# Two matmul bursts of a scan made one: the B^T x products of a Mamba-2 chunk scan written beside its C.B products

## The chip, the cores and the metric

The kernel runs on one core of a Trainium2 chip. A core has a matrix engine (TensorE, PE in the profile; its weight loads are PEld), a vector engine (DVE), a scalar engine (ACT), GpSimd (POOL) and a sync engine (SP) that issues DMAs. Each engine takes its own instructions in the order in which they were written. Matmul results land in PSUM, which has eight banks of 2 KB in each of 128 partitions; everything else lies in SBUF. The metric is the device time of one execution in microseconds (us).

## The reference

A chunked state-space scan feeds a feed-forward layer. All is float32, four sequences of 768 steps, 8 heads, head size 32, state size 16. The recurrence is linear, so the chunk length is a choice of the kernel.

```python
for c in range(nc):                                  # per chunk, every batch b and head h
    cum = np.cumsum(log_a[chunk]); L = exp(cum_i - cum_j) * causal
    CB = einsum('bhin,bhjn->bhij', Cc, Bc)
    y_intra = einsum('bhij,bhjd->bhid', CB * L, xc)
    y_inter = einsum('bhin,bhnd->bhid', Cc, state) * exp(cum)
    y[chunk] = y_intra + y_inter
    Bx = Bc (outer) xc * exp(cum_last - cum)
    state = exp(sum(la)) * state + sum_j(Bx)
x = y as (3072, 256)
h = x @ w_in                                         # 256 -> 2048
out = (h * sigmoid(h)) @ w_out                       # 2048 -> 256
```

## The kernel before, in words

The 3072 rows are cut into 12 units of 256 steps, three to a sequence; a unit holds four chunks of 64 steps. The kernel works on three units at a time: in round g it runs the first layer of unit g (`f_s1`), the scan of unit g+1, and the second layer of unit g-2 (`f_s2`). A round has eight slots j, and in each slot the code writes down, in this order, an eighth of `f_s1`, a piece of the scan, in the first two rounds a piece of the weights (`next_w`), and from round 2 on an eighth of `f_s2`. No scheduler reorders it. So the order in the code is the order in every engine's queue, and semaphores hold an instruction until its inputs are there and its buffer is free.

The scan of a unit has five pieces. `f_P` and `f_E` (slot 0) make the decays on DVE with some small POOL steps; `f_T` and `f_B` (slot 1) transpose B and C on PE and scale B by the decays on POOL (the tile BT); `f_G` (slot 2) forms the C.B products, 16 matmuls into the four PSUM banks of the tile gy, and DVE multiplies them by the decays (the tile M); `f_D` (slot 4) forms the B^T x products, 16 matmuls (12 in the last unit of a sequence), and DVE runs the state recurrence over them (the tiles st, then sp); `f_Y` (slot 6) forms the scan's output, 16 (or 12) matmuls from sp and 32 from M, and ACT copies it to SBUF as XM, the input of `f_s1` one round later.

PSUM is full: the pool `ps_s` has one buffer of four banks (gy, shared in turn by the C.B products and the scan's output), `ps_h` has two buffers of one bank (hp), and `ps_o` two for the second layer. hp serves the first layer's results, the transposes and the B^T x products in turn. `f_D` takes both hp buffers at once, one for each half c of the 128 partitions of x (L278 writes `dp[c]`).

The weights are not used as they arrive. Each of 16 pieces (8 of w_in, 8 of w_out) passes ACT (L136, L138), POOL (L141), DVE (L146), POOL (L147) and DVE (L152) in the first two rounds, one piece per slot and step.

A float32 matmul shows up as two records in the trace, so 16 matmuls are 32 records, and an eighth of a layer (four matmuls of 256 columns) is 8 records.

Of the kernel before, what the change touches and what calls it, by code (L numbers as in the profile page):

```python
# [7 lines left out]
FP32 = mybir.dt.float32  # L8
# [11 lines left out]
def kernel(  # L20
# [20 lines left out]
    nc = tc.nc  # L41
# [5 lines left out]
    UPB = S // UT  # L47
# [15 lines left out]
    ps_h = ctx.enter_context(tc.tile_pool(name="ps_h", bufs=2, space=bass.MemoryType.PSUM))  # L63
# [5 lines left out]
    pa, ab, bct, xt = {}, {}, {}, {}  # L69
# [130 lines left out]
    for i in range(2):  # L200
        t = const.tile([128, UT], FP32, name=f"pb{i}")
# [3 lines left out]
    E, M, BT, BH, CE, CW, PFX, ST, DP, XM, GTS, OPS = ({} for _ in range(12))  # L205


    def f_P(u):

        t, s = pa.pop(u), pb[u % 2]  # L210
        nc.vector.tensor_scalar(out=t, in0=t, scalar1=1.0, scalar2=1e-6, op0=ALU.min, op1=ALU.max)  # L211
        starts = t.rearrange("p (c t) -> p c t", t=Q)[:, :, 0:1]
        nc.gpsimd.tensor_copy(out=s.rearrange("p (c t) -> p c t", t=Q)[:, :, 0:1], in_=starts)  # L213
        nc.gpsimd.memset(starts, 0.0)
        PFX[u] = sc.tile([128, UT], FP32, name="pfx")
        nc.vector.tensor_tensor_scan(out=PFX[u], data0=t, data1=s, initial=0.0, op0=ALU.mult, op1=ALU.add)

    def f_E(u):
        t = ab.pop(u)
        nc.vector.tensor_scalar(out=t, in0=t, scalar1=1.0, scalar2=1e-6, op0=ALU.min, op1=ALU.max)  # L220
        nc.gpsimd.memset(t[:, :, :, 0:1], 0.0)  # L221
        E[u] = sc.tile([128, 2, H, Q], FP32, name="E")
        nc.vector.tensor_tensor_scan(out=E[u].rearrange("p k h t -> p (k h t)"),  # L223
                                     data0=t.rearrange("p k h t -> p (k h t)"),
                                     data1=diag.rearrange("p g t -> p (g t)"),
                                     initial=0.0, op0=ALU.mult, op1=ALU.add)

    def f_B(u):

        BT[u] = sc.tile([128, 2, H, N], FP32, name="BT")  # L230
        nc.gpsimd.tensor_tensor(out=BT[u], in0=bct[u][:, 0], in1=E[u][:, :, :, Q - 1:Q].to_broadcast([128, 2, H, N]),
                                op=ALU.mult)

    def f_T(u):

        tp = ps_h.tile([128, 4, 128], FP32, name="hp")
        for i in range(2):
            for k in range(2):
                nc.tensor.transpose(out=tp[:, 2 * i + k], in_=bct[u][:, i, k].rearrange("p h n -> p (h n)"),  # L239
                                    identity=ident)  # L240
        BH[u] = sc.tile([128, UT], FP32, name="bh")
        CE[u] = sc.tile([128, 2, UT], FP32, name="ce")
        CW[u] = sc.tile([128, UT], FP32, name="cw")
        tb = tp[:, 0:2].rearrange("p k t -> p (k t)")
        tcc = tp[:, 2:4].rearrange("p k t -> p (k t)")
        nc.scalar.activation(BH[u], tb, AF.Copy)
        for e in range(2):
            nc.scalar.activation(CE[u][:, e], tcc, AF.Copy, scale=par[:, e:e + 1])  # L248
        nc.vector.tensor_tensor(out=CW[u], in0=tcc, in1=PFX[u], op=ALU.mult)  # L249

    def f_G(u):
        bh, ce = BH.pop(u), CE.pop(u)
        gram = ps_s.tile([128, 4, 512], FP32, name="gy")
        for k in range(2):
            for c in range(2):
                ts = slice(128 * k + 64 * c, 128 * k + 64 * c + 64)
                for g in range(4):
                    nc.tensor.matmul(out=gram[64 * c:64 * c + 64, g, 128 * k:128 * k + 128],  # L258
                                     lhsT=bh[32 * g:32 * g + 32, ts], rhs=ce[32 * g:32 * g + 32, :, ts],
                                     start=True, stop=True, tile_position=(32 * g, 64 * c), skip_group_check=True)  # L260
        M[u] = sc.tile([128, 2, 4, 2 * Q], FP32, name="M")
        nc.vector.tensor_tensor(out=M[u].rearrange("p k g x -> p g k x"),  # L262
                                in0=gram[:, :, 0:256].rearrange("p g (k x) -> p g k x", k=2),
                                in1=E[u].rearrange("p k (g e) t -> p g k (e t)", e=2), op=ALU.mult)

    def f_D(u):

        first, last = u % UPB == 0, u % UPB == UPB - 1
        bt = BT.pop(u).rearrange("p k h n -> p k (h n)")
        xc = xt[u].rearrange("p k h d -> p k (h d)")  # L270
        E.pop(u)
        bct.pop(u)
        dp = [ps_h.tile([128, 512], FP32, name="hp") for c in range(2)]
        n = 3 if last else 4
        for t in range(n):
            k, c = divmod(t, 2)
            for g in range(4):
                nc.tensor.matmul(out=dp[c][32 * g:32 * g + 32, 64 * k:64 * k + 64],  # L278
                                 lhsT=bt[64 * c:64 * c + 64, k, 32 * g:32 * g + 32],
                                 rhs=xc[64 * c:64 * c + 64, k, 64 * g:64 * g + 64], start=True, stop=True,  # L280
                                 tile_position=(64 * c, 32 * g), skip_group_check=True)
        if first:
            ST[u] = sc.tile([128, 4, 64], FP32, name="st")
        if not last:
            ST[u + 1] = sc.tile([128, 4, 64], FP32, name="st")
        for t in range(n):
            k, c = divmod(t, 2)
            o = ST[u][:, t + 1] if t < 3 else ST[u + 1][:, 0]
            d = dp[c][:, 64 * k:64 * k + 64]
            if first and t == 0:  # L290
                nc.vector.tensor_copy(out=o, in_=d)
            else:
                nc.vector.scalar_tensor_tensor(out=o, in0=ST[u][:, t], scalar=PFX[u][:, Q * t + Q - 1:Q * t + Q],  # L293
                                               in1=d, op0=ALU.mult, op1=ALU.add)

        s0 = 1 if first else 0
        sp = DP[u] = sc.tile([128, 4, 64], FP32, name="sp")
        nc.vector.tensor_tensor(out=sp[:, s0:], in0=ST.pop(u)[:, s0:],  # L298
                                in1=hmask.rearrange("p e d -> p (e d)").rearrange("p (o x) -> p o x", o=1)
                                .to_broadcast([128, 4 - s0, 64]), op=ALU.mult)  # L300
        PFX.pop(u)

    def f_Y(u):
        first = u % UPB == 0
        sp, cw, m, xc = DP.pop(u), CW.pop(u), M.pop(u), xt.pop(u)
        m = m.rearrange("p k g (e t) -> p k (g e) t", e=2)

        y = ps_s.tile([128, 4, 512], FP32, name="gy")
        for t in range(1 if first else 0, 4):
            k, c = divmod(t, 2)  # L310
            for g in range(4):
                w, q = divmod(g, 2)
                nc.tensor.matmul(out=y[64 * q:64 * q + 64, 2 * w + c, 64 * k:64 * k + 64],  # L313
                                 lhsT=sp[32 * g:32 * g + 32, t], rhs=cw[32 * g:32 * g + 32, Q * t:Q * t + Q],
                                 start=(k == 0 or (first and t == 2)), stop=False,
                                 tile_position=(32 * g, 64 * q), skip_group_check=True)
        for k in range(2):
            for w in range(2):
                for c in range(2):
                    for q in range(4):  # L320
                        h = 4 * w + q
                        nc.tensor.matmul(out=y[32 * q:32 * q + 32, 2 * w + c, 64 * k:64 * k + 64],  # L322
                                         lhsT=xc[64 * c:64 * c + 64, k, h], rhs=m[64 * c:64 * c + 64, k, h],
                                         start=False, stop=True, tile_position=(64 * c, 32 * q),
                                         skip_group_check=True)

        XM[u] = sc.tile([128, 4, 128], FP32, name="XM")
        nc.scalar.activation(XM[u], y[:, :, 0:128], AF.Copy)
# [31 lines left out]
    def scan_piece(u, j):  # L360
        if j == 0:
            f_P(u)
            f_E(u)
        elif j == 1:
            f_T(u)
            f_B(u)
        elif j == 2:
            f_G(u)
        elif j == 4:
            f_D(u)  # L370
        elif j == 6:
            f_Y(u)
        elif j == 7 and u + 2 < NU:
            load_unit(u + 2)
# [4 lines left out]
    f_T(0)  # L379
    f_B(0)  # L380
    next_w(0)
    f_G(0)
    next_w(1)
    f_D(0)
    next_w(2)
    f_Y(0)
    next_w(3)
# [42 lines left out]
```

## Time and profile before

| what | value |
|---|---|
| time, median of 3 runs (range) | 435.57 us (435.03 to 436.4) |
| time of the profiled execution | 433.9 us |
| its span, first to last instruction | 432.2 us |
| PE busy | 385.3 us, 89% of the span |
| DVE / ACT / POOL busy | 113.8 / 106.9 / 71.2 us |
| mean granted TensorE clock | 0.988 of 2.4 GHz |
| first layer, PE (L339) | 187.9 us in 768 records |
| second layer, PE (L350) | 181.7 us in 768 records |
| B^T x products, PE (L278) | 8.5 us in 352 records, 9.9 us idle before them |
| POOL, in 40 slices of the span | busy in the first 8, idle after |

"Idle before" is the time in which the engine stood still just ahead of these instructions. The profile has two stages: a ramp of some 89 us in which the weights are prepared, and a stage of some 310 us in which each round repeats.

### The profile page before, as it was taken

How to read it: one execution, taken by the hardware profiler on the slowest of the kernel's cores; microseconds unless marked ns; L12 is line 12 of the kernel's file. 1: busy time of each engine (PE TensorE's matmuls, PEld its weight loads, DVE VectorE, ACT ScalarE, POOL GpSimd, SP SyncE). 2: the span in 40 equal slices, each digit the busy share in tenths (PEclk: the TensorE clock that was granted, in tenths of full speed). 3: DMA queues.
4: the chain of work that ended last, by engine and by line, in shares of the span. 5: the costliest groups of instructions: out<-in, count | busy, mean ns of one | idle time of the engine just before them, and what ended most of it. 6: DMA issues, size and time to landing. Idle time of an engine off the chain costs nothing.

```text
span 432.2 us, 7900 instructions
## 1 busy us (share of the span) xinstructions
PE 385.3 (89%) x3440; PEld 323.9 (75%) x3440; DVE 113.8 (26%) x162; ACT 106.9 (25%) x202; POOL 71.2 (16%) x95
## 2 busy tenths in 40 slices
PE   2255785799999999999999999999999999999996
PEld 1144563688888888888888888887887887888885
DVE  1728868813212213113014014014014011000000
ACT  2254564131221222222222221221222221221000
POOL 4567988500000000000000000000000000000000
PEclk9998998899999999999999999999999999999999
DMA  9969469402502403303304305205200000000101
GB/s 160 170 222 198 164 170 198 52 0 51 73 14 66 57 14 75 48 14 79 51 6 89 47 3 94 42 2 93 44 0 14 14 2 12 14 9 4 24 14 24
DMA packets 110082, 26.20 MB, mean 61 GB/s; under 512 B 101344, under 2 KB 105952, under 8 KB 110048
## 3 DMA queue, kind: packets, MB, share of 16 engines
q1 hardware_dynamic: 103808, 25.18, 29.0%
q10 hardware_dynamic: 6240, 0.52, 1.2%
q8 instruction: 27, 0.44, 0.4%
q14 instruction: 7, 0.06, 0.1%
HBM read 22.54 MB, written 3.15 MB: 59 GB/s over the span
## 4 chain that ended last, share of the span: by engine, by line
PE 79%; POOL 9%; DMA 4%; SPq 2%; issue 2%; ACT 2%; ACTq 1%; DVE 1%; POOLq 0%; DVEq 0%
PE o_ps L350 40%; PE hp L339 34%; POOL wu L141 6%; POOL wv L147 3%; PE gy L322 2%; DMA xt<-in_x_dram 2%; PE gy L313 1%; PE gy L258 1%; ACT gT L341 1%; DMA raw<-in_moe_w_in_dram 1%; SPq L93 1%; PE hp L239 1%; PE hp L278 1%; DMA ab<-in_a_dram 1%; ACTq L93 1%
## 5 line engine op out<-in xcount | busy, mean ns | idle before, releaser
L339 PE MATMUL hp<-XM,w_in_sb 128*128 128x256 f32 x768 | 187.9, 390 | 20.2 <-DVE w_in_sb L152 6.2
L339 PEld LDWEIGHTS hp<-XM,w_in_sb 128*128 128x128 f32 x768 | 149.4, 196 | 43.7 <-issue 9.5
L350 PE MATMUL o_ps<-w_out_sb,gT 128*128 128x256 f32 x768 | 181.7, 383 | 0.0
L350 PEld LDWEIGHTS o_ps<-w_out_sb,gT 128*128 128x128 f32 x768 | 143.0, 190 | 21.2 <-issue 1.5
L341 ACT ACTIVATE gT<-hp 128x512 f32<-128x512 f32 x96 | 57.2, 596 | 231.0 <-PE hp L339 231.0
L249 DVE TENSOR_TENSOR cw<-hp,pfx 128x256 f32<-128x256 f32 x12 | 5.0, 421 | 124.0 <-ACT ce L248 124.0
L213 POOL COPY pb<-pa 128x4 f32<-128x4 f32 x12 | 2.3, 191 | 207.2 <-DVE pa L211 207.2
L141 POOL TENSOR_SCALAR wu<-wu 128x512 f32<-128x512 f32 x16 | 32.8, 2054 | 6.4 <-ACT wu L136 6.4
L223 DVE TENSOR_TENSOR_SCAN E<-ab,diag 128x1024 f32<-128x1024 f32 x12 | 28.3, 2355 | 2.6 <-POOL ab L221 2.6
L293 DVE SCALAR_TENSOR_TENSOR st<-st,pfx,hp 128x64 f32<-128x64 f32 x40 | 11.2, 281 | 43.5 <-PE hp L278 41.8
L147 POOL TENSOR_TENSOR wv<-wu,wv 128x512 uint32<-128x512 uint32 x16 | 21.3, 1333 | 3.2 <-DVE wu L146 3.2
L355 ACT ACTIVATE o_sb<-o_ps 128x256 f32<-128x256 f32 x24 | 9.2, 383 | 49.8 <-PE o_ps L350 49.8
L262 DVE TENSOR_TENSOR M<-gy,E 128x1024 f32<-128x1024 f32 x12 | 14.7, 1223 | 24.6 <-PE gy L258 24.6
L146 DVE TENSOR_SCALAR wu<-wu 128x512 uint32<-128x512 uint32 x16 | 16.8, 1053 | 12.4 <-POOL wu L141 12.4
L278 PE MATMUL hp<-xt,BT 64*32 64x64 f32 x352 | 8.5, 234 | 9.9 <-ACT gT L341 6.5
L278 PEld LDWEIGHTS hp<-xt,BT 64*32 64x32 f32 x352 | 4.7, 109 | 15.7 <-ACT gT L341 8.3
L136 ACT ACTIVATE wu<-raw 128x512 f32<-128x512 f32 x16 | 10.7, 669 | 16.1 <-DMA raw<-in_moe_w_in_dram 12.7
L239 PE MATMUL hp<-ident,bct 128*128 128x128 f32 x48 | 8.2, 288 | 6.9 <-DMA bct<-in_B_dram 4.0
L313 PEld LDWEIGHTS gy<-cw,sp 32*64 32x64 f32 x352 | 6.5, 138 | 8.5 <-issue 8.5
L138 ACT ACTIVATE wv<-raw 128x512 f32<-128x512 uint32 x16 | 10.6, 666 | 8.7 <-DVE w_out_sb L152 5.6
L239 PEld LDWEIGHTS hp<-ident,bct 128*128 128x128 f32 x48 | 6.2, 145 | 8.7 <-DMA bct<-in_C_dram 3.2
L313 PE MATMUL gy<-cw,sp 32*64 32x64 f32 x352 | 8.2, 230 | 4.6 <-DVE sp L298 4.6
(33 smaller groups left out, 116.9 us busy)
## 6 DMA issues: line engine op xcount, KB each, us to landing
ab<-in_a_dram SPq DMA_DIRECT2D x48, 128.0 KB, 4.0
raw<-in_moe_w_in_dram SPq DMA_DIRECT2D x8, 512.0 KB, 6.8
raw<-in_moe_w_out_dram SPq DMA_DIRECT2D x8, 512.0 KB, 4.4
out_dram<-o_sb SPq DMA_DIRECT2D x48, 64.0 KB, 1.9
xt<-in_x_dram SPq DMA_DIRECT2D x22, 128.0 KB, 3.0
pa<-in_a_dram SPq DMA_DIRECT2D x12, 128.0 KB
bct<-in_B_dram SPq DMA_DIRECT2D x22, 64.0 KB, 3.6
bct<-in_C_dram SPq DMA_DIRECT2D x22, 64.0 KB, 3.5
```

Of the source, the lines that this page charges most:

```text
L141: nc.gpsimd.tensor_scalar(out=u, in0=u, scalar1=LEAST, scalar2=MOST, op0=ALU.max, op1=ALU.min)
L146: nc.vector.tensor_scalar(out=u, in0=u, scalar1=3, scalar2=None, op0=ALU.logical_shift_left)
L147: nc.gpsimd.tensor_tensor(out=v, in0=u, in1=v, op=ALU.add)
L223: nc.vector.tensor_tensor_scan(out=E[u].rearrange("p k h t -> p (k h t)"), data0=t.rearrange("p k h t -> p (k h t)"), data1=diag.rearrange ...
L239: nc.tensor.transpose(out=tp[:, 2 * i + k], in_=bct[u][:, i, k].rearrange("p h n -> p (h n)"), identity=ident)
L262: nc.vector.tensor_tensor(out=M[u].rearrange("p k g x -> p g k x"), in0=gram[:, :, 0:256].rearrange("p g (k x) -> p g k x", k=2), in1=E[u] ...
L278: nc.tensor.matmul(out=dp[c][32 * g:32 * g + 32, 64 * k:64 * k + 64], lhsT=bt[64 * c:64 * c + 64, k, 32 * g:32 * g + 32], rhs=xc[64 * c:64 ...
L293: nc.vector.scalar_tensor_tensor(out=o, in0=ST[u][:, t], scalar=PFX[u][:, Q * t + Q - 1:Q * t + Q], in1=d, op0=ALU.mult, op1=ALU.add)
L313: nc.tensor.matmul(out=y[64 * q:64 * q + 64, 2 * w + c, 64 * k:64 * k + 64], lhsT=sp[32 * g:32 * g + 32, t], rhs=cw[32 * g:32 * g + 32, Q ...
L339: nc.tensor.matmul(out=hp[:, i], lhsT=w_in_sb[:, kc, f * 128:(f + 1) * 128], rhs=xm[:, kc], start=(kc == 0), stop=(kc == KC - 1))
L341: nc.scalar.activation(GTS[g][:, 2 * j:2 * j + 2], hp, AF.Silu)
L350: nc.tensor.matmul(out=OPS[g], lhsT=GTS[g][:, f, 128 * c:128 * c + 128], rhs=w_out_sb[:, f, :], start=(f == 0), stop=(f == NF - 1))
```

## The change

The B^T x matmuls no longer get buffers of their own. The C.B products fill columns 0 to 255 of each 512-column bank of the tile gy; the B^T x products of half c now go into columns 256 to 383 of bank c of the same tile. Both sets of matmuls are issued as one burst in slot 2 (`f_GD`), and DVE then does M, st and sp one behind the other. The scan's output burst (`f_Y`) moves from slot 6 to slot 5. Ahead of the rounds, for unit 0, the one burst stands where `f_D` stood.

```diff
-    def f_G(u):
+    def f_GD(u):
...
         gram = ps_s.tile([128, 4, 512], FP32, name="gy")
...
+        for t in range(n):
+            k, c = divmod(t, 2)
+            for g in range(4):
+                nc.tensor.matmul(out=gram[32 * g:32 * g + 32, c, 256 + 64 * k:320 + 64 * k],
+                                 lhsT=bt[64 * c:64 * c + 64, k, 32 * g:32 * g + 32],
+                                 rhs=xc[64 * c:64 * c + 64, k, 64 * g:64 * g + 64], start=True, stop=True,
+                                 tile_position=(64 * c, 32 * g), skip_group_check=True)
         M[u] = sc.tile([128, 2, 4, 2 * Q], FP32, name="M")
...
-    def f_D(u):
...
-        dp = [ps_h.tile([128, 512], FP32, name="hp") for c in range(2)]
...
-                nc.tensor.matmul(out=dp[c][32 * g:32 * g + 32, 64 * k:64 * k + 64],
...
-            d = dp[c][:, 64 * k:64 * k + 64]
+            d = gram[:, c, 256 + 64 * k:320 + 64 * k]
...
-            f_G(u)
-        elif j == 4:
-            f_D(u)
-        elif j == 6:
+            f_GD(u)
+        elif j == 5:
             f_Y(u)
...
-    f_G(0)
     next_w(1)
-    f_D(0)
+    f_GD(0)
     next_w(2)
```

On PE, in a round with all three parts (round 2, slot 4 before), the B^T x matmuls L278 stand between the two layers, in two parts with a wait for ACT between them:

```order
L339 MATMUL hp<-XM,w_in_sb 128x256 [waits Activation_49]
L339 MATMUL hp<-XM,w_in_sb 128x256 x3
L278 MATMUL hp<-xt,BT 32x64 [waits DMAHW0_49,Activation_49,Pool_49]
L278 MATMUL hp<-xt,BT 32x64 x3
L278 MATMUL hp<-xt,BT 32x64 [waits Activation_49]
L278 MATMUL hp<-xt,BT 32x64 x3
L278 MATMUL hp<-xt,BT 32x64 [waits DMAHW1_49]
L278 MATMUL hp<-xt,BT 32x64 x7
L350 MATMUL o_ps<-w_out_sb,gT 128x256 x4
L339 MATMUL hp<-XM,w_in_sb 128x256 [waits DVE_49,PE_49]
```

In the changed kernel they stand in slot 2 of the same round, right behind the C.B matmuls (L263, L258 before), and are L269; first and second layer are L337 and L348:

```order
L263 MATMUL gy<-ce,bh 64x128 [waits Activation_49]
L263 MATMUL gy<-ce,bh 64x128 x15
L269 MATMUL gy<-xt,BT 32x64 [waits DMAHW0_49,Pool_49]
L269 MATMUL gy<-xt,BT 32x64 x7
L269 MATMUL gy<-xt,BT 32x64 [waits DMAHW1_49]
L269 MATMUL gy<-xt,BT 32x64 x7
L348 MATMUL o_ps<-w_out_sb,gT 128x256 [waits DVE_49]
L348 MATMUL o_ps<-w_out_sb,gT 128x256
L348 MATMUL o_ps<-w_out_sb,gT 128x256 [waits DVE_49]
```

The B^T x matmuls have lost both waits for ACT and keep those for POOL (BT) and for the load of x.

On DVE, in the ramp (round 0, slots 2 to 4, unit 1), the state recurrence (st, sp) stood behind four steps of the weights, two of L146 and two of L152:

```order
L262 TENSOR_TENSOR M<-gy,E 128x4x2x128 [waits DVE_49,PE_49]
L146 TENSOR_SCALAR wu<-wu 128x512 [waits Pool_49]
L152 SCALAR_TENSOR_TENSOR w_in_sb<-raw,wv 128x2x256 [waits DMAHW2_49,Pool_49]
L146 TENSOR_SCALAR wu<-wu 128x512 [waits DVE_49,Pool_49]
L152 SCALAR_TENSOR_TENSOR w_in_sb<-raw,wv 128x2x256 [waits DMAHW3_49,Pool_49]
L293 SCALAR_TENSOR_TENSOR st<-st,pfx,hp 128x64 [waits PE_49]
L293 SCALAR_TENSOR_TENSOR st<-st,pfx,hp 128x64 [waits DVE_49,PE_49]
L293 SCALAR_TENSOR_TENSOR st<-st,pfx,hp 128x64 [waits DVE_49] x2
L298 TENSOR_TENSOR sp<-st,hmask 128x256
```

Now it stands right behind M, ahead of these steps; the first st has no wait for PE of its own, so the wait of M is for the whole burst:

```order
L274 TENSOR_TENSOR M<-gy,E 128x4x2x128 [waits DVE_49,PE_49]
L291 SCALAR_TENSOR_TENSOR st<-st,pfx,gy 128x64
L291 SCALAR_TENSOR_TENSOR st<-st,pfx,gy 128x64 [waits DVE_49] x3
L296 TENSOR_TENSOR sp<-st,hmask 128x256
L146 TENSOR_SCALAR wu<-wu 128x512 [waits Pool_49]
L152 SCALAR_TENSOR_TENSOR w_in_sb<-raw,wv 128x2x256 [waits DMAHW2_49,Pool_49]
L146 TENSOR_SCALAR wu<-wu 128x512 [waits Pool_49]
L152 SCALAR_TENSOR_TENSOR w_in_sb<-raw,wv 128x2x256 [waits DMAHW3_49,Pool_49]
```

Of a unit's DVE steps in the ramp, st and sp moved up past four steps of the weights.

## Rows read from the trace of the kernel before

**Rows 1.** Windows: us, PE, PEld, DVE, ACT, POOL busy (instructions), granted clock, DMA, GB/s

```profile
88.71:399.00 310.29, 306.33 (x2696) 260.37 (x2695) 57.21 (x92) 69.13 (x135) 8.48 (x32) 1.00 0.20 36
68.30:73.50 5.20, 5.17 (x20) 4.07 (x20) 4.53 (x4) 2.56 (x5) 5.20 (x5) 0.70 0.85 245
```

**Rows 2.** Waits of PE from 92 to 400 us: total, times, longest

```profile
PE hp L278 <- ACT gT L341: 4.0, 9, 0.4
```

**Rows 3.** Timeline of PE, round 2, and its end: start, us, records, [idle before <- releaser]

```profile
96.15 0.69 PE L258 MATMUL gy<-ce,bh 32*64 32x128 f32 x32
96.77 1.99 PE L350 MATMUL o_ps<-w_out_sb,gT 128*128 128x256 f32 x8
...
102.06 1.89 PE L339 MATMUL hp<-XM,w_in_sb 128*128 128x256 f32 x8
103.88 0.32 PE L278 MATMUL hp<-xt,BT 64*32 64x64 f32 x8
104.63 0.43 PE L278 MATMUL hp<-xt,BT 64*32 64x64 f32 x24 [0.44 <-ACT gT L341]
104.99 1.99 PE L350 MATMUL o_ps<-w_out_sb,gT 128*128 128x256 f32 x8
106.82 1.89 PE L339 MATMUL hp<-XM,w_in_sb 128*128 128x256 f32 x8
...
398.54 29.52 PE L350 MATMUL o_ps<-w_out_sb,gT 128*128 128x256 f32 x136
```

**Rows 4.** Timeline of PE, round 4, a last unit of a sequence

```profile
165.55 1.89 PE L339 MATMUL hp<-XM,w_in_sb 128*128 128x256 f32 x8
...
168.13 0.35 PE L278 MATMUL hp<-xt,BT 64*32 64x64 f32 x16 [0.44 <-ACT gT L341]
168.40 1.99 PE L350 MATMUL o_ps<-w_out_sb,gT 128*128 128x256 f32 x8
```

**Rows 5.** Timeline of PE, the output burst of round 3

```profile
143.78 0.69 PE L313 MATMUL gy<-cw,sp 32*64 32x64 f32 x32
144.41 0.86 PE L322 MATMUL gy<-M,xt 64*32 64x64 f32 x64
```

**Rows 6.** Timeline of PE in the ramp, round 1 and the start of round 2

```profile
63.69 0.69 PE L258 MATMUL gy<-ce,bh 32*64 32x128 f32 x32
68.33 5.21 PE L339 MATMUL hp<-XM,w_in_sb 128*128 128x256 f32 x16 [3.95 <-DVE cw L249]
...
75.94 0.35 PE L278 MATMUL hp<-xt,BT 64*32 64x64 f32 x16 [2.15 <-ACT gT L341]
78.66 5.16 PE L339 MATMUL hp<-XM,w_in_sb 128*128 128x256 f32 x16 [2.37 <-DVE st L293]
83.74 0.69 PE L313 MATMUL gy<-cw,sp 32*64 32x64 f32 x32
...
88.71 1.89 PE L350 MATMUL o_ps<-w_out_sb,gT 128*128 128x256 f32 x8
```

**Rows 7.** Timeline of DVE in the ramp, round 0

```profile
41.80 1.23 DVE L262 TENSOR_TENSOR M<-gy,E 128x1024 f32<-128x1024 f32 x1 [1.91 <-PE gy L258]
42.94 0.84 DVE L146 TENSOR_SCALAR wu<-wu 128x512 uint32<-128x512 uint32 x1
...
47.63 1.30 DVE L293 SCALAR_TENSOR_TENSOR st<-st,pfx,hp 128x64 f32<-128x64 f32 x4 [0.29 <-PE hp L278]
48.84 0.78 DVE L298 TENSOR_TENSOR sp<-st,hmask 128x256 f32<-128x256 f32 x1
```

**Rows 8.** Timeline of POOL in the ramp: a weight step, BT of units 2 and 3

```profile
44.77 1.27 POOL L147 TENSOR_TENSOR wv<-wu,wv 128x512 uint32<-128x512 uint32 x1
...
69.04 0.81 POOL L231 TENSOR_TENSOR BT<-bct,E 128x256 f32<-128x256 f32 x1
...
87.63 0.64 POOL L231 TENSOR_TENSOR BT<-bct,E 128x256 f32<-128x256 f32 x1 [2.46 <-DVE E L223]
```

**Rows 9.** Timeline of ACT ahead of round 0

```profile
24.84 0.66 ACT L136 ACTIVATE wu<-raw 128x512 f32<-128x512 f32 x1 [8.94 <-DMA raw<-in_moe_w_in_dram]
```

More of the change, by code (lines that the diff above doesn't have):

```diff
@@ L249, in f_T @@
         nc.vector.tensor_tensor(out=CW[u], in0=tcc, in1=PFX[u], op=ALU.mult)
-    def f_G(u):
+    def f_GD(u):
+        first, last = u % UPB == 0, u % UPB == UPB - 1
         bh, ce = BH.pop(u), CE.pop(u)
+        bt = BT.pop(u).rearrange("p k h n -> p k (h n)")
+        xc = xt[u].rearrange("p k h d -> p k (h d)")
+        n = 3 if last else 4
         gram = ps_s.tile([128, 4, 512], FP32, name="gy")
@@ L264, in f_G @@
                                 in1=E[u].rearrange("p k (g e) t -> p g k (e t)", e=2), op=ALU.mult)
-    def f_D(u):
-        first, last = u % UPB == 0, u % UPB == UPB - 1
-        bt = BT.pop(u).rearrange("p k h n -> p k (h n)")
-        xc = xt[u].rearrange("p k h d -> p k (h d)")
         E.pop(u)
         bct.pop(u)
-        dp = [ps_h.tile([128, 512], FP32, name="hp") for c in range(2)]
[L274 to L277, printed above, removed]
-                nc.tensor.matmul(out=dp[c][32 * g:32 * g + 32, 64 * k:64 * k + 64],
-                                 lhsT=bt[64 * c:64 * c + 64, k, 32 * g:32 * g + 32],
-                                 rhs=xc[64 * c:64 * c + 64, k, 64 * g:64 * g + 64], start=True, stop=True,
-                                 tile_position=(64 * c, 32 * g), skip_group_check=True)
         if first:
```

## The prediction

> **What bounds the kernel now.** I first read busy time by windows. From 88.71 us, where the second layer starts, to 399 us PE is busy 306.33 of 310.29 us at full granted clock [rows 1]. PE is the bound there, so only PE's own time and its waits count. The list of who waited for whom then says what the missing 4 us are: nine waits of 0.44 us, one per round, each of the B^T x matmuls for ACT's silu, which frees the second hp buffer [rows 2]. The timeline of PE gives the price of each piece of a round [rows 3 to 5]. Ahead of 88.71 us PE is not the bound; it follows the weights, which go through POOL and DVE, and there I read the timeline of each engine [rows 6 to 8]. From 78.66 us on PE runs without a gap into the steady stage [rows 6]. So the end moves with two things: when PE stops waiting in the ramp, and what a round costs after.
>
> **The steady rounds.** Nine units (3 to 11) have their B^T x products in rounds where PE is the bound. The yardstick is eight records of a layer: 29.52 us / 136 x 8 = 1.73 us [rows 3].
> What goes. The first-layer eighth that starts at 102.06 is done at 103.79; the next layer's work starts at 104.99, so the products cost 1.20 us, and the eighth behind them takes 106.82 - 104.99 = 1.83 instead of 1.73, 0.10 more [rows 3]. Sum 1.30. In a last unit of a sequence (three of the nine): 168.40 - 165.55 - 1.73 = 1.12, plus 0.10, 1.22 [rows 4].
> What comes. Behind the C.B matmuls the products run in one piece. 24 records take 104.99 - 104.63 = 0.36 from first start to the start of what follows [rows 3], 16 take 0.27 [rows 4], so 8 more cost 0.09: 0.45 for 32 records, 0.36 for 24. The C.B matmuls' own 0.62 (96.15 to 96.77) and the slower eighth behind a burst stay, since a burst is still there [rows 3].
> Saved: 1.30 - 0.45 = 0.85 for six units, 1.22 - 0.36 = 0.86 for three, together 7.7 us.
> Bounds. If the products in the burst took what their two parts take today without the wait, 0.32 + 0.36 = 0.68, and another 0.07 for the join, each unit would save 0.55, 5.0 us in all. If nothing but the nine waits went, 4.0 us. If the switch inside the burst were free and only the 0.09 per 8 records counted (0.36), 8.6 us. I take 7.7, since the 24-record row is the same instruction without a wait.
> The joint in the burst needs a look. The C.B matmuls use 32*64 tiles of the array, the products 64*32. The output burst makes the same change today: 32 records of the first kind take 143.78 to 144.41, 0.63 us, before the second kind starts, and the C.B matmuls take 0.62 before a full-array matmul starts [rows 3, 5]. So that change costs as much as a change to the full array, which the 0.62 holds already. The Trainium skill (TensorEngine Tiling (Array Packing), Key Properties) says that changing the tiling mode drains the engine, which speaks against a mixed burst. If that drain came on top, say the 0.10 seen behind a burst, the steady gain would be 0.9 us less, 6.8; the rows here say it is inside.
> Covers. In the steady stage M starts one product burst (0.45) later and st and sp follow it: 1.23 + 1.30 + 0.78 us at most [rows 7]. The output burst, now in slot 5, has six eighths of layers in front of it (10.4 us), so sp and M are ready. The products need BT earlier than before. The tightest is unit 3: its BT is done at 88.27 and its C.B burst starts at 96.15 [rows 3, 8], 7.9 us of cover; moving PE forward by what the ramp gives still leaves some 4. With that cover gone the whole core would wait for BT.
>
> **The ramp.** Unit 0: the burst moves behind one weight step on DVE, and M with it, some 1 to 3 us. ACT, which must copy this unit's output, stands idle 8.94 us until 24.84 for a weight load that is ahead of the copy in its queue [rows 9]. That hides it.
> Unit 1 (round 0): M now waits for the products too, some 0.45 us, starts near 42.2 and is followed by st and sp: 42.2 + 1.23 + 1.30 + 0.4 to 0.8 puts the weight step of 42.94 at 45.1 to 45.6 [rows 7]. POOL's next step stood ready behind it at 44.77 [rows 8]; with the weight step's 0.4 to 0.8 us it starts near 45.9. POOL takes the weight steps one behind the other from there, so the weight chain and what is queued in it run about 1.1 us late (bounds 0, and 2.8 with every DVE step at its longest). In exchange PE loses its waits around the old products in round 0, which decide nothing, as the weights set the pace.
> Unit 2 (round 1) decides. Today PE waits for DVE until 68.33, for ACT until 75.94 and for st until 78.66 [rows 6]. The last two waits exist only because the products need both hp buffers and give them back late. In the changed kernel PE, at the end of its C.B matmuls (64.38), waits for BT, which POOL has at 69.85 [rows 6, 8], plus 1.1: 70.95. Behind that wait stand all later matmuls. The products end near 71.5. What then stands before the second layer: two eighths of the first layer after a long idle, which today take 5.21 at a granted clock of 0.70 [rows 1, 6]; one more, 1.73; the output burst and two eighths, 88.71 - 83.74 = 4.97 [rows 6]; and a last one, 1.73. Sum 13.6, so the second layer starts at 85.1 instead of 88.71: 3.6 us earlier. Late next would be ACT's silus, which queue behind weight steps; that none of them is late no row can show, and rival A is the price.
> Bounds: without POOL's delay and with the clock at its high level (2 x 1.73 for 5.21) the gain is 3.6 + 1.1 + 1.7 = 6.4; with the delay at 2.8 it is 1.9, and one more slow restart (1.7) leaves 0.2.
>
> **Sum.** 7.7 + 3.6 = 11.3 us off. The profiled execution took 433.9 us (span 432.2 and 1.7 around it), so it would take 422.6. The median of the runs shown, 435.57, lies 1.67 above; the time that I forecast is 435.57 - 11.3 = 424.3.
>
> **Rivals.**
> A. The ramp gives nothing: PE resumes earlier but meets new waits, for BT and then for silus behind late weight steps, that eat it up. For it: three engines' queues are coupled there, and DVE's 3 us now stand ahead of weight steps. Against: the two waits of 2.15 and 2.37 lose their reason [rows 6]. Then 435.57 - 7.7 = 427.9.
> B. The burst is no cheaper than its parts and only the waits go: 4.0 + 3.6 = 7.6, 428.0. For it: the array still changes its tiling twice. Against: rows 3 and 5, as above.
> C. Slower. The products share banks 0 and 1 of gy with what DVE reads as M. If they were held until M has been read, or the hardware held them, each steady burst would stand still for DVE's start-up and M, 0.1 + 1.23 [rows 7] and 0.1 to restart: 1.45 x 9 = 13.0 us, against 11.3 gained: 437.3. It decides from 1.26 us per burst on. Against it: the order of the changed kernel shows the products waiting for x and BT alone, and M behind them.
> D. No change: BT late by the whole gain. The weight chain would have to come 11 us late at unit 2, where I count 1.1. About 435.5.
>
> **Chances.** My sum with its own bounds 0.64, A 0.15, B 0.12, C 0.05, D 0.04. For my sum's own range the steady part lies between 5.0 and 8.1 and the ramp between 1.9 and 6.2, 6.9 to 14.3 off: 421.3 to 428.7, which takes in A and B; I trim it to 421.5 and 428.5. Faster by over 0.3% (1.3 us, about what can be told from no change here) 0.91, within it 0.04, slower 0.05.
>
> **What would show it.** In the profile after: no wait of the products for ACT, each steady round shorter by 0.85 us, products behind the C.B matmuls in 0.45 us, a PE wait for BT of 5 to 7 us in round 1, and the second layer starting near 85 us. A steady wait for POOL or DVE at the burst, or a second layer that starts at 88 us or later, would prove a step wrong.

## The result, and the profile after

The changed kernel takes 423.5 us (median of 4 runs, 422.91 to 424.47) against 435.64 us before (435.03 to 436.4): 12.1 us off, ratio 0.9723 with a 95% interval of 0.9698 to 0.9748. The forecast was 424.3. In a second job it took 423.05 us against 435.16, ratio 0.9719 (0.969 to 0.9747).

The profiled executions took 433.9 us before and 423.86 after, which is 10.0 apart and not 12.1: the one of before lay 1.7 us under its median, the one of after 0.4 above. The stages below come from these two executions.

I cut each at three starts that PE's timeline gives: the first record of the first layer, of the second layer, and the last row of 136 records. Before, the first is this row, the second stands at 88.71 [rows 6] and the third at 398.54 [rows 3].

```profile
26.58 5.67 PE L339 MATMUL hp<-XM,w_in_sb 128*128 128x256 f32 x16 [5.03 <-ACT XM L328]
```

After, in the timeline of PE (start, us, records, [idle before <- releaser]):

```profile
27.70 6.19 PE L337 MATMUL hp<-XM,w_in_sb 128*128 128x256 f32 x16 [5.00 <-ACT XM L326]
...
65.80 0.69 PE L263 MATMUL gy<-ce,bh 32*64 32x128 f32 x32
72.02 0.65 PE L269 MATMUL gy<-xt,BT 64*32 64x64 f32 x24 [5.52 <-POOL BT L231]
72.60 7.62 PE L337 MATMUL hp<-XM,w_in_sb 128*128 128x256 f32 x24
80.15 0.69 PE L311 MATMUL gy<-cw,sp 32*64 32x64 f32 x32
...
86.84 1.89 PE L348 MATMUL o_ps<-w_out_sb,gT 128*128 128x256 f32 x8
...
94.28 0.69 PE L263 MATMUL gy<-ce,bh 32*64 32x128 f32 x32
94.90 0.45 PE L269 MATMUL gy<-xt,BT 64*32 64x64 f32 x32
95.29 1.99 PE L348 MATMUL o_ps<-w_out_sb,gT 128*128 128x256 f32 x8
...
156.54 0.43 PE L269 MATMUL gy<-xt,BT 64*32 64x64 f32 x24
156.90 1.99 PE L348 MATMUL o_ps<-w_out_sb,gT 128*128 128x256 f32 x8
...
388.49 29.52 PE L348 MATMUL o_ps<-w_out_sb,gT 128*128 128x256 f32 x136
```

The ramp (first to second start) went from 88.71 - 26.58 = 62.13 us to 86.84 - 27.70 = 59.14; the steady stage from 309.83 to 301.65. That is 3.0 and 8.2 us. The first layer itself began 1.1 us later after; what it waited for, ACT's copy behind a weight load, is the same in both, and its start lay anywhere from 25.3 to 27.9 us in the kernels below, so I count that as chance: the load let ACT go at 24.84 before [rows 9] and at 25.96 after, e1, with the order of before up to there, started at 27.32 and e2, with the changed order, at 26.71. 3.0 + 8.2 - 1.1 = 10.0 with rounding, the difference of the spans. The medians, 12.1 apart, leave 12.1 - 8.2 = 3.9 us for the ramp and the first layer's start together; the 3.0 is what this one pair of executions shows.

The reader is to see two things in the rows. In the steady burst the products follow the C.B matmuls without a wait, and the second layer follows 0.39 us (24 records: 0.36) later. In the ramp the waits of 3.95, 2.15 and 2.37 us behind the C.B burst of unit 2 [rows 6] are gone and one of 5.52 us for BT stands there. The windows of the same execution (us, PE, PEld, DVE, ACT, POOL busy, granted clock, DMA, GB/s) say that PE is never idle in the steady stage, and that after the long wait it ran at a mean clock of 0.71:

```profile
72.60:80.15 7.55, 7.55 (x29) 6.01 (x25) 6.81 (x9) 3.57 (x6) 7.55 (x5) 0.71 0.97 161
72.60:76.10 3.50, 3.50 (x12) 2.85 (x9) 3.26 (x6) 1.24 (x2) 3.50 (x3) 0.50 1.19 253
86.84:388.49 301.65, 301.65 (x2693) 259.72 (x2692) 58.66 (x93) 68.93 (x134) 9.29 (x34) 1.00 0.21 37
```

The weight chain in round 0, on DVE and then on POOL, after:

```profile
43.38 1.23 DVE L274 TENSOR_TENSOR M<-gy,E 128x1024 f32<-128x1024 f32 x1 [2.35 <-PE gy L269]
44.52 1.22 DVE L291 SCALAR_TENSOR_TENSOR st<-st,pfx,gy 128x64 f32<-128x64 f32 x4
45.66 0.42 DVE L296 TENSOR_TENSOR sp<-st,hmask 128x256 f32<-128x256 f32 x1
46.00 0.42 DVE L146 TENSOR_SCALAR wu<-wu 128x512 uint32<-128x512 uint32 x1
```

```profile
46.50 1.65 POOL L147 TENSOR_TENSOR wv<-wu,wv 128x512 uint32<-128x512 uint32 x1 [0.57 <-DVE wu L146]
...
71.15 0.81 POOL L231 TENSOR_TENSOR BT<-bct,E 128x256 f32<-128x256 f32 x1
```

POOL's step that stood at 44.77 [rows 8] is at 46.50, BT of unit 2 at 71.15 instead of 69.04; less the 1.1 us of the late start, 0.6 and 1.0 us late.

In round 1 a slow restart of PE went too, not only waiting. Before, PE came back at the lower clock twice, at 68.33 [rows 1, 6] and at 78.66, where these are the windows of before:

```profile
78.66:82.00 3.34, 3.34 (x9) 2.75 (x10) 2.51 (x4) 0.00 (x0) 2.58 (x3) 0.56 0.59 86
82.00:83.70 1.70, 1.70 (x9) 1.25 (x7) 0.90 (x2) 0.60 (x1) 0.63 (x3) 1.00 0.00 0
```

After, it did so once. From the C.B burst of unit 2 to the second layer the kernel before took 88.71 - 63.69 = 25.0 us, the changed one 86.84 - 65.80 = 21.0: some 3.0 less of waits (8.47 against 5.52) and 1.0 less for the six eighths of the first layer in between (13.79 against 12.83). The burst itself started 1.0 us later, counted from the first layer's start, which leaves the 3.0.

### The profile page after: what moved, and what is told of

It reads as the page before. It is cut to its first block, busy times and chain, and to the rows that moved or that the text cites. A ratio compares the mean times of both kernels' runs of the same rounds, so it can differ in the third digit from the quotient of the medians.

```text
span 422.2 us, 7871 instructions
## 1 busy us (share of the span) xinstructions
PE 380.5 (90%) x3440; PEld 323.2 (77%) x3440; DVE 111.8 (26%) x162; ACT 107.3 (25%) x202; POOL 71.7 (17%) x95
## 4 chain that ended last, share of the span: by engine, by line
PE 83%; POOL 6%; DMA 4%; SPq 2%; issue 2%; DVE 1%; ACTq 1%; ACT 0%; POOLq 0%; DVEq 0%
PE o_ps L348 40%; PE hp L337 36%; POOL wu L141 3%; POOL wv L147 2%; DMA xt<-in_x_dram 2%; PE gy L320 2%; PE gy L263 2%; PE gy L311 1%; DMA raw<-in_moe_w_in_dram 1%; PE gy L269 1%; SPq L93 1%; PE hp L239 1%; DMA ab<-in_a_dram 1%; ACTq L93 1%; SPq L84 0%
## 5 line engine op out<-in xcount | busy, mean ns | idle before, releaser
L337 PE MATMUL hp<-XM,w_in_sb 128*128 128x256 f32 x768 | 186.9, 389 | 15.0 <-DVE w_in_sb L152 6.9
L348 PE MATMUL o_ps<-w_out_sb,gT 128*128 128x256 f32 x768 | 180.7, 381 | 0.0
L337 PEld LDWEIGHTS hp<-XM,w_in_sb 128*128 128x128 f32 x768 | 148.7, 195 | 38.4 <-issue 5.4
L348 PEld LDWEIGHTS o_ps<-w_out_sb,gT 128*128 128x128 f32 x768 | 143.7, 190 | 20.1
L141 POOL TENSOR_SCALAR wu<-wu 128x512 f32<-128x512 f32 x16 | 32.9, 2056 | 6.4 <-ACT wu L136 6.4
L146 DVE TENSOR_SCALAR wu<-wu 128x512 uint32<-128x512 uint32 x16 | 17.5, 1095 | 14.0 <-POOL wu L141 14.0
L269 PE MATMUL gy<-xt,BT 64*32 64x64 f32 x352 | 5.8, 238 | 9.5 <-POOL BT L231 9.5
L269 PEld LDWEIGHTS gy<-xt,BT 64*32 64x32 f32 x352 | 3.7, 115 | 12.0 <-POOL BT L231 10.1
L231 POOL TENSOR_TENSOR BT<-bct,E 128x256 f32<-128x256 f32 x12 | 8.0, 671 | 24.6 <-DVE E L223 19.6
```

The costliest lines, as they stand in the source:

```text
L141: nc.gpsimd.tensor_scalar(out=u, in0=u, scalar1=LEAST, scalar2=MOST, op0=ALU.max, op1=ALU.min)
L146: nc.vector.tensor_scalar(out=u, in0=u, scalar1=3, scalar2=None, op0=ALU.logical_shift_left)
L269: nc.tensor.matmul(out=gram[32 * g:32 * g + 32, c, 256 + 64 * k:320 + 64 * k], lhsT=bt[64 * c:64 * c + 64, k, 32 * g:32 * g + 32], rhs=xc[ ...
L337: nc.tensor.matmul(out=hp[:, i], lhsT=w_in_sb[:, kc, f * 128:(f + 1) * 128], rhs=xm[:, kc], start=(kc == 0), stop=(kc == KC - 1))
L348: nc.tensor.matmul(out=OPS[g], lhsT=GTS[g][:, f, 128 * c:128 * c + 128], rhs=w_out_sb[:, f, :], start=(f == 0), stop=(f == NF - 1))
```

## The experiments

Each ran for several executions beside the kernel before. The stages are cut as above, from one profiled execution each.

| kernel | median us | ratio to before (95%) | ramp | steady |
|---|---|---|---|---|
| before | 435.64 | | 62.13 | 309.83 |
| changed (two jobs) | 423.5, 423.05 | 0.9723 (0.9698 to 0.9748), 0.9719 (0.969 to 0.9747) | 59.14, 60.31 | 301.65, 301.79 |
| e1 free columns alone | 425.12 | 0.9765 (0.9739 to 0.9792) | 58.97 | 303.43 |
| e2 joined burst alone | 428.47 | 0.9846 (0.9826 to 0.9866) | 61.85 | 303.44 |
| e3, e11 output burst in slot 6 | 425.1, 423.77 | 0.9765 (0.9744 to 0.9785), 0.9726 (0.9703 to 0.9749) | 60.39, 60.23 | 301.65, 301.65 |
| e4 PE kept busy | 421.16 | 0.9682 (0.9662 to 0.9703) | 57.44 | 301.75 |
| e6 decays earlier | 426.23 | 0.9781 (0.9751 to 0.981) | 61.42 | 301.65 |
| e7 more weight buffers | 423.12 | 0.9723 (0.9702 to 0.9744) | 60.43 | 301.65 |
| e8 e6 and e7 | 421.93 | 0.9678 (0.9653 to 0.9704) | 57.41 | 301.71 |
| e9 scan a slot earlier | 423.37 | 0.9717 (0.9695 to 0.9739) | 55.42 | 306.75 |
| e10 weights held back | 422.63 | 0.9702 (0.9681 to 0.9723) | 55.42 | 305.65 |
| e12 e8, PE kept busy | 419.29 | 0.962 (0.9593 to 0.9646) | 56.92 | 301.65 |

**e1, the free columns without the joined burst.** Edit against the changed kernel: the products and the state steps go back into a function `f_D` of their own in slot 4, `f_Y` into slot 6; the products still write into gy.

```diff
-            f_GD(u)
-        elif j == 5:
+            f_G(u)
+        elif j == 4:
+            f_D(u)
+        elif j == 6:
             f_Y(u)
```

> The free columns alone: the B^T x products go into columns 256 to 383 of the C.B tile, but keep their own burst in slot 4, and the output burst stays in slot 6. Theory (both the freed hp buffers and the joined burst pay): the 0.44 us wait for ACT and the two-part run go, but a burst of its own costs 0.09 to start, 0.45 to run and 0.10 behind it, 0.64 instead of 1.30, so 9 x 0.66 = 5.9 us in the steady rounds; in the ramp PE no longer waits for hp in round 1, but the output burst waits for sp, second layer at about 85 us, 3.5 us off; about 426. Rival (it is only the buffers): as fast as the changed kernel, 423.5. Rival (it is only the burst): no faster than before, 435.6.

PE's timeline in round 2:

```profile
99.63 1.89 PE L341 MATMUL hp<-XM,w_in_sb 128*128 128x256 f32 x8
101.45 0.46 PE L277 MATMUL gy<-xt,BT 64*32 64x64 f32 x32
101.84 1.99 PE L352 MATMUL o_ps<-w_out_sb,gT 128*128 128x256 f32 x8
103.67 1.89 PE L341 MATMUL hp<-XM,w_in_sb 128*128 128x256 f32 x8
```

No wait, 0.39 us for the products, 0.09 to get into the burst (101.45 - 99.63 - 1.73) and 0.10 behind it (103.67 - 101.84 - 1.73). The steady stage is 6.4 us shorter than before, the theory said 5.9; joining the bursts is worth the other 1.8, which is 0.2 for each of nine units. The ramp gains as much as in the changed kernel, as said, and the output burst in it waits 2.46 us for sp. The rival that only the buffers count is 1.8 us off in the trace; by the times alone, whose intervals against the changed kernel's overlap, it could not be told.

**e2, the joined burst without the free columns.**

```diff
+        dp = [ps_h.tile([128, 512], FP32, name="hp") for c in range(2)]
...
-                nc.tensor.matmul(out=gram[32 * g:32 * g + 32, c, 256 + 64 * k:320 + 64 * k],
+                nc.tensor.matmul(out=dp[c][32 * g:32 * g + 32, 64 * k:64 * k + 64],
...
-            d = gram[:, c, 256 + 64 * k:320 + 64 * k]
+            d = dp[c][:, 64 * k:64 * k + 64]
```

> The joined burst alone: C.B and B^T x products in one burst in slot 2, output burst in slot 5, but the B^T x products still go into the two hp buffers. Theory: the wait for ACT is mostly hidden behind the C.B matmuls, but DVE reads M (1.23 us) before st, so hp comes back 0.1 + 1.23 + 0.9 = 2.2 us after the burst while only 1.73 us of second layer cover it; a steady unit waits some 0.5 to 0.6 us for st and saves 0.3, 2 to 3 us over nine units; the ramp no better than before or worse; 431 to 435. Rival (the burst is what pays): 9 x 0.85 = 7.7 us in the steady rounds, about 425.

PE in round 2, then DVE:

```profile
96.62 0.56 PE L270 MATMUL hp<-xt,BT 64*32 64x64 f32 x32
97.12 1.99 PE L349 MATMUL o_ps<-w_out_sb,gT 128*128 128x256 f32 x8
99.00 1.96 PE L338 MATMUL hp<-XM,w_in_sb 128*128 128x256 f32 x8
```

```profile
96.80 1.23 DVE L275 TENSOR_TENSOR M<-gy,E 128x1024 f32<-128x1024 f32 x1 [2.52 <-PE gy L263]
```

My theory was wrong for the steady stage. With the products in another tile M waits for the C.B matmuls alone and starts at 96.80, while the products still run, so st is early enough: the wait behind it is 0.05 us (99.00 - 97.12 against 1.83), not 0.5. The products take 0.50 instead of 0.39. So the joined burst alone also saves 6.4 us in the steady stage: it puts the C.B matmuls (from 96.00) over the time in which ACT frees the buffer (its silu runs from 96.11 to 96.71). It gains next to nothing in the ramp (61.85 against 62.13), where PE waits for st, 1.88 us in round 0 and 1.63 us in round 1, besides 5.51 us for BT. So either part of the change takes away the nine waits; the ramp gain is the free columns' alone. The medians agree: e2 is 6.3 us under the kernel before timed beside it, its steady gain and no more, e1 9.7, some 3.3 more than its steady gain.

**e3 and e11, the output burst back in slot 6.** One number (5 to 6); the same kernel in two jobs.

> The changed kernel with the output burst back in slot 6. Theory: the slot of the output burst does nothing, since sp and M are ready by slot 5 and first-layer work lies around it either way; same time as the changed kernel within 0.5 us, 423.5. Rival (the earlier output burst is part of the gain, as XM comes sooner): 1 us or more slower, 424.5 to 426.

> The changed kernel with the output burst in slot 6, once more, since its first time (425.1) lay above the changed kernel's in another job (423.05, 423.5), while its trace shows the same steady stretch (301.65 us). Theory: the slot of the output burst is worth at most the wait that it fills in round 0; 423.5 to 424.5. Rival (slot 5 is worth more than 1 us): 424.8 to 425.5.

The first time it looked 0.4% slower than the changed kernel, the second time not (0.9726 against 0.9719 to 0.9723), and the steady stage is the same to 0.01 us. No effect of the slot is shown, so the slot does not explain the 1.8 us by which e1's steady stage is longer either.

**e4, PE kept busy in the wait for BT.**

```diff
+    FILL = 11
...
+        if u == 2:
+            fill = ps_o.tile([128, d_model], FP32, name="o_ps")
+            for i in range(FILL):
+                nc.tensor.matmul(out=fill, lhsT=w_in_sb[:, 0, 0:128], rhs=w_in_sb[:, 0, 0:256], start=True, stop=True)
```

> The changed kernel with 11 matmuls of 256 columns (22 records, 4.8 us) without use written into a free o_ps buffer between the C.B and the B^T x products of unit 2 alone, so that PE does not stand idle for 5.5 us there. Theory: the 24 records behind the wait for BT took 7.55 us where 5.18 are due at full clock, because the granted clock fell to its lower level in the idle time; kept busy, PE keeps its clock and 2.0 to 2.4 us go, about 421.3. Rival (the records are slow for another reason, such as waits for silus or operands): no change, 423.5, or up to 0.5 slower.

PE in round 1, and the window of the 24 records:

```profile
67.00 5.02 PE L270 MATMUL o_ps<-w_in_sb 128*128 128x256 f32 x22
72.60 0.43 PE L274 MATMUL gy<-xt,BT 64*32 64x64 f32 x24 [0.58 <-POOL BT L232]
72.95 5.45 PE L342 MATMUL hp<-XM,w_in_sb 128*128 128x256 f32 x24
```

```profile
72.95:78.33 5.38, 5.38 (x31) 4.48 (x24) 4.79 (x9) 2.97 (x5) 5.38 (x4) 1.00 1.23 269
```

5.38 us at a granted clock of 1.00 instead of 7.55 at 0.71: 2.2 us, and the median is 1.9 to 2.3 below the changed kernel's. By the ratios to the kernel before, each in its own job, it is 1.6 to 1.8 us, and the intervals just touch, so the times alone would not carry it. DVE and POOL are busy for the same share of the window as there. The price of the clock is shown by the trace.

**e5, the changed kernel again.**

> The changed kernel itself, timed beside the three that follow. Theory: 423.5 again (422.5 to 424.5); in its trace the stretch from the second layer's start to the last round of the first layer is 301.6 us as in its first profile, and the ramp about 59 us from the first layer's start. Rival (the first profile was a lucky one): second layer a microsecond or more later.

As said, but for the ramp, 60.31 instead of 59.14: the same kernel's ramp differs by a microsecond between executions. The windows of PE's eighth behind its wait in round 0, in the first execution and then in this one, show where that comes from:

```profile
38.71:41.66 2.95, 2.95 (x9) 1.94 (x9) 2.32 (x3) 0.58 (x1) 2.95 (x3) 0.63 0.86 100
38.88:42.56 3.68, 3.68 (x8) 2.49 (x8) 2.31 (x3) 0.57 (x1) 3.68 (x3) 0.50 1.04 165
```

Here the granted clock stayed at 0.50 for the whole eighth (3.68 us instead of 2.95), and the burst behind it took 1.70 us instead of 1.50. Counted from the first layer's start, M, POOL's step and BT of unit 2 all came 0.9 us later, and the three eighths behind BT took 7.82 us instead of 7.55. That is the whole difference of the two ramps.

**e6, e7, e8, what else holds the ramp.** In e6 `f_P` and `f_E` of the next unit stand in slot 6 and `f_B` in slot 7 of the round before; in e7 the pools of the weights are larger; e8 has both.

```diff
+        if j == 6 and u + 1 < NU:
+            f_P(u + 1)
+            f_E(u + 1)
+        if j == 7 and u + 1 < NU:
+            f_B(u + 1)
```

```diff
-    rawp = ctx.enter_context(tc.tile_pool(name="rawp", bufs=5))
-    wtp = ctx.enter_context(tc.tile_pool(name="wtp", bufs=3))
+    rawp = ctx.enter_context(tc.tile_pool(name="rawp", bufs=7))
+    wtp = ctx.enter_context(tc.tile_pool(name="wtp", bufs=6))
...
-    RAW = 5
+    RAW = 7
```

> The changed kernel with the decays (f_P, f_E) of the next unit written in slot 6 of the round before and BT in slot 7, instead of slots 0 and 1, so that BT of unit 2 is ready before its burst. Theory: the 5.5 us wait for BT goes, but the decays now delay weight steps, and ACT's silus queue behind those (buffers of the weight tiles), so most of the wait comes back as PE waits for ACT; 1 to 3 us off, 420.5 to 422.5. Rival (BT alone holds the ramp): 5 us and more off, 418.5 or less.

> The changed kernel with more buffers for the weights (7 instead of 5 for what is loaded, 6 instead of 3 for the tiles between the steps), so that ACT's weight steps do not hold the silus behind them. Theory: PE still waits for BT of unit 2 in round 1, as BT hangs on POOL and DVE; no gain, 423 to 424. Rival (the silus are what holds the ramp): 2 us or more off, 421.5 or less.

> e6 and e7 together: decays and BT a slot or two earlier, and more buffers for the weights. Theory: with both couplings gone PE runs round 1 without the 5.5 us wait for BT, keeps its clock (2.4 us), and the ramp is bounded by the weights themselves; 5 to 8 us off, 415.5 to 418.5, faster than both kernels. Rival (POOL's weight steps hold the second layer anyway, as the last piece must be there): no more than 2 us off, 421.5 or above.

PE in round 1, e6, then e7, then e8:

```profile
64.71 0.66 PE L239 MATMUL hp<-ident,bct 128*128 128x128 f32 x4 [3.08 <-ACT gT L339]
67.17 3.57 PE L337 MATMUL hp<-XM,w_in_sb 128*128 128x256 f32 x8 [1.80 <-ACT gT L339]
...
71.30 0.43 PE L269 MATMUL gy<-xt,BT 64*32 64x64 f32 x24
...
79.21 2.42 PE L337 MATMUL hp<-XM,w_in_sb 128*128 128x256 f32 x8 [3.84 <-ACT gT L339]
```

```profile
71.71 0.65 PE L269 MATMUL gy<-xt,BT 64*32 64x64 f32 x24 [7.11 <-POOL BT L231]
```

```profile
66.34 0.43 PE L269 MATMUL gy<-xt,BT 64*32 64x64 f32 x24 [0.52 <-POOL BT L231]
71.53 7.00 PE L337 MATMUL hp<-XM,w_in_sb 128*128 128x256 f32 x24 [4.76 <-DVE cw L249]
```

ACT in e6, ahead of the last of these waits:

```profile
77.47 0.66 ACT L136 ACTIVATE wu<-raw 128x512 f32<-128x512 f32 x1 [6.02 <-DMA raw<-in_moe_w_out_dram]
78.03 0.65 ACT L138 ACTIVATE wv<-raw 128x512 f32<-128x512 uint32 x1
78.59 0.57 ACT L339 ACTIVATE gT<-hp 128x512 f32<-128x512 f32 x1
```

In e6 the wait for BT is gone, and PE waits 8.7 us for silus that queue behind weight steps on ACT. The longest of these waits, 3.84 us, hangs on a load and not on another engine's pace: the weight step ahead of the silu stood 6.02 us until its piece of w_out was loaded. The kernel is 3.2 us slower than e5, where I had said 1 to 3 faster. e7 gives nothing, as said: the silus come sooner, and the wait for BT is just longer. e8 has 0.52 us left of the wait for BT and no wait for silus in round 1 above 0.25 us, but one of 4.76 us for cw, which on DVE stands behind weight steps; it is 1.1 us faster than e5 by the medians, far from the 5 to 8 forecast, and the two intervals overlap. The rival's time came true, but not its reason: the last piece of the weights did not hold the second layer, as e9 and e10 start it 2 us sooner. The wait moves from engine to engine. I read this as round 1 being held by the order of the scan's steps among the weight steps, which go at POOL's pace, 3.3 us a piece (its L141 starts at 48.12, 51.42, 54.73 and 58.02 in the changed kernel); no run with a faster POOL shows it.

**e9 and e10, later orders.** Both build on e8. e9 moves the scan of units 2 to 11 a slot up; e10 also writes the last four weight pieces' steps two slots later.

```diff
+        elif j == 0:
+            f_T(u)
         elif j == 1:
-            f_T(u)
-            f_B(u)
-        elif j == 2:
             f_GD(u)
-        elif j == 5:
+        elif j == 4:
             f_Y(u)
...
-            if 8 * g + j + 4 < len(W) + 2:
-                next_w(8 * g + j + 4)
+            if g == 0:
+                next_w(j + 4)
+            elif g == 1 and j >= 2:
+                next_w(j + 10)
```

The weight lines are e10's alone; it also writes the decays of units 3 to 11 in slot 3 and BT in slot 4.

> e8 with the scan of units 2 to 11 one slot earlier (transposes in slot 0, the joined burst in slot 1, output burst in slot 4), as in e8 the wait of 4.76 us for cw has taken the place of the wait for BT: cw stood on DVE behind weight steps that wait for POOL. Theory (DVE's order against the weight steps holds the ramp): cw comes one weight step (3.3 us) earlier, the output burst then waits for sp behind the next weight step; 2 to 3 us off e8, 419 to 420. Rival (something else, such as POOL's own rate, sets the second layer's start): same as e8, 421.5 to 422.5.

> e9, and the weight steps of pieces 12 to 15 written two slots later, behind the burst of unit 2, with the decays of units 3 to 11 in slot 3 and BT in slot 4 of the round before. Theory: DVE does cw, M, st and sp of unit 2 ahead of weight steps that are not urgent; PE runs round 1 with waits of about 3 us instead of about 5 to 8, second layer near 80 to 82 us instead of 85; 417 to 419. Rival (the last weight pieces then come too late for the second layer, PE waits for w_out in round 2): 421 or more.

PE in round 2, e9, then e10:

```profile
88.39 0.46 PE L269 MATMUL gy<-xt,BT 64*32 64x64 f32 x32 [3.45 <-POOL BT L231]
```

```profile
91.57 3.59 PE L337 MATMUL hp<-XM,w_in_sb 128*128 128x256 f32 x8 [2.29 <-DVE cw L249]
```

Both start the second layer 2 us sooner than e8 (ramp 55.42), and give it back in round 2, where unit 3 now waits: the steady stage is 5.1 and 4.0 us longer. Not faster than e8 or, beyond their intervals, the changed kernel. Both forecasts fell; the gain was lost to the next unit's wait and a clock that fell once more in it (mean granted clock 0.52 from 91.57 to 94.99 in e10, 0.70 from 88.39 to 94.02 in e9).

**e12, e8 with PE kept busy.** The lines of e4, 10 matmuls, behind the joined burst.

> e8 (decays and BT of the next unit earlier, more weight buffers) and the filling of e4: 10 matmuls without use (20 records, 4.3 us) behind the joined burst of unit 2, where PE in e8 waits 4.76 us for cw and then takes 7.00 us for 24 records. Theory (the granted clock falls in that wait): the 24 records take 5.4 to 5.5 us, 1.5 us off e8, about 420.4, and 2.5 to 3 us off the changed kernel. Rival (the two do not add, as DVE and POOL hold the ramp): as e8, 421.9 or above.

```profile
66.55 4.58 PE L276 MATMUL o_ps<-w_in_sb 128*128 128x256 f32 x20
71.38 5.45 PE L341 MATMUL hp<-XM,w_in_sb 128*128 128x256 f32 x24 [0.24 <-DVE cw L249]
...
83.89 1.89 PE L352 MATMUL o_ps<-w_out_sb,gT 128*128 128x256 f32 x8
```

The 24 records take 5.45 us instead of 7.00. 419.29 us, ratio 0.962 (0.9593 to 0.9646), is faster than both kernels; its interval lies clear of the changed kernel's. By the medians the two edits add up, 2.6 us off e8 where 1.5 was forecast. The trace has those 1.5 us in the 24 records; its ramp is only 0.5 us shorter than e8's, because BT came 0.6 us later after the first layer's start and the output burst waited 0.36 us for sp. It is the slowest of e12's five executions (420.95 us), and where the other microsecond of the medians comes from is not shown.

## Why the prediction was right

**The bound and the nine waits.** Right. PE bounds the steady stage; the waits of 0.44 us are gone and nothing took their place: PE is busy in all of 301.65 us.

**The steady sum.** 7.7 forecast, 8.2 measured. The burst was sized right: 0.36 for 24 records to the hundredth, and 0.39 for 32 where I had 0.45, as 8 more records cost 0.03 and not the 0.09 between my rows of 16 and 24. With 0.39 the sum is 8.0. e1 splits the 8.2: 6.4 for the wait and the two parts, 1.8 for one burst less. So rival B is out, and a burst of small tiles between the layers costs 0.2 us to enter and leave: 0.09 and 0.10 for the products alone in e1, and as much for the C.B burst before (96.15 - 94.33 - 1.73 and 98.60 - 96.77 - 1.73, the eighths around it starting at 94.33, 96.77 and 98.60). The doubt about the joint in the burst is settled too: the change from 32*64 to 64*32 costs nothing above the 0.62 us of the C.B matmuls (94.28 to 94.90). The Trainium skill (TensorEngine Tiling (Array Packing), Key Properties) has a change of tiling mode drain the engine. No run here shows a drain by itself; the trace shows that this change takes as long as the one to the full array.

**The covers.** Right. No steady burst waits for BT, M or sp; BT of unit 3, the tightest, was done at 90.07 and used at 94.90, 4.8 us of cover.

**The ramp.** The mechanism held step by step. Counted from the first layer's start, the weight chain ran 0.6 to 1.0 us late (1.1 forecast; 1.5 to 1.9 in e5's execution), BT of unit 2 held PE for 5.52 us, and the products ended at 72.60 - 1.12 = 71.48 (71.5 forecast). The term that was mis-sized is the restart: 5.21 + 1.73 = 6.9 us for the three eighths, 7.55 measured. I took the row of a stretch behind an idle time of 3.95 us; behind 5.52 us with only the products in between, the clock stayed at its lower level (0.50 of 2.4 GHz) for at least 3.5 us of the eighths. From there to the second layer 6.69 us, forecast 6.70. The ramp gave 3.0 instead of 3.6 in this execution, 1.8 in the second one, measured against a single execution of before. The 1.2 us between the two are the granted clock in round 0 and behind BT (e5), which the forecast took as given. That one of before's two slow restarts goes is in the sum without being named: it has one slow stretch after, where round 1 of before had two. And PE's pace in round 0, whose waits the forecast let decide nothing, does count: M follows PE there, and the weight chain follows M.

**What I had not separated.** I credited the freed buffers with the steady gain's waits. e2 shows that the joined burst takes them away as well, and that only the ramp needs the free columns. Each part alone gives 6.4 us in the steady stage and both together 8.2, so the two do not add.

**The other rivals.** A is out as it stood: the ramp gains, though its wait for BT did come, and e4 shows a further 2.2 us that the slow restart behind that wait costs. C is out: no burst was held for M; M was held for the burst, as the order said. D needed 11 us of lateness, 1.0 came.

**What stays open.** Why the first layer starts anywhere between 25.3 and 27.9 us, and why the clock in round 0 differs between executions, was not tried. How far an order of weight and scan steps could shorten the ramp is open as well; e9 and e10 show that moving single steps moves the wait.

## What to carry to other kernels

Where a small burst borrows buffers that the main stream cycles through, look for room in a bank that the program already holds: the wait at the borrowing and the late return go together, and the burst can then join another one, which saves its entry and exit as well. Where there is no room, joining the burst to another can hide the wait by itself (e2). Cost such a change separately in each stage: here a wait that was taken away in the steady stage was gone, while in the ramp, which follows the weights, it reappeared one step later, on another engine. And price a long idle time of PE with the slow restart behind it.

## What the runs showed of the hardware that was not expected

Useless matmuls made the kernel faster: 22 records in a wait of 5.5 us bought 2.2 us, since the granted clock stayed at 1.00 instead of 0.50 for the 3.5 us that followed (e4, and again 1.5 us in e12). And the first layer's start, which hangs on the third weight load, varied by up to 2.5 us between kernels that are alike up to there (26.2 to 27.9 us in the changed kernel, e3, e4, e6 and e11; 25.3 to 27.7 in e7 to e10 and e12, which have more weight buffers), more than several of the effects studied. The granted clock in one eighth of round 0, 0.63 or 0.50 in two executions of the same kernel, moved the second layer by most of a microsecond, though PE is not the bound there (e5).
